# Regrouping the small attention matmuls of a packed-attention and mixture-of-experts kernel by array tile

## The chip, the cores and the metric

One core of one Trainium2 chip runs the whole program. The metric is the time of one execution in device microseconds, lower is better. In the profile PE is TensorE's matmuls, PEld its weight loads, DVE VectorE, ACT ScalarE, POOL GpSimd and SP SyncE (here a queue of DMA issues). A line number after L is a line of the kernel before, unless the text says that it is one of the changed kernel.

## What is computed

```python
# per batch (8) and head (8): q, k, v are [576, 64], p is [32, 64]
p_packed = softmax(scale * p @ k.T) @ v                       # [32, 64]
x        = softmax(scale * q @ p_packed.T) @ p_packed         # [576, 64]
# x of all heads side by side: 4608 tokens of 512
xn, en   = x / (norm(x) + 1e-6), emb / (norm(emb) + 1e-6)     # emb: 8 experts of 512
logits   = xn @ en.T / tau
e        = argmax(logits)                                     # one expert per token
out      = softmax(logits)[e] * (relu(x @ w1[e]) @ w2[e])     # w1 [512,1024], w2 [1024,512]
```

## The kernel before

**Work per batch.** The program goes through the 8 batches. For each it guesses one expert for the whole batch from the packed values (`pair_sums`, `guess_products`, `guess`), loads that expert's w1 and w2, and runs the feed-forward part (`ffn`) on all 576 tokens with it; tokens that want another expert would be done in a loop at the end, which these inputs do not enter.

**Groups and tiles.** The 8 heads of a batch form two groups g of four. Column tile `c` (32 of the array's 128 columns) holds head `head(g, c) = c ^ g`. A matmul's `tile_position` says which rows and columns of the array it takes; an operand of 64 rows and 32 columns leaves room for eight such matmuls side by side, one of 128 rows and 32 columns for four.

**The attention of one batch**, in TensorE's order:

1. `key_scores` (L266): scores of the 32 packed rows of each head against 576 keys; `key_max` on DVE, `key_exp` on ACT give `p1[g]`, 128 rows (4 heads of 32) by 576 keys.
2. `p1_turn` (L374): five transposes per group, four of 128 keys and one of the last 64, here called the odd block. `p1_evac` copies the four blocks (L385 on ACT, or L387 on DVE) and the odd one (L388 on DVE) to `p1T[g]`.
3. `pack_values` (L394): for each group 5 blocks by 4 heads, weights `p1T`, moving 64 columns of v. The odd block uses 64 rows of the array, the others 128.
4. `pair_rows` on DVE (L406), `pair_turn` on PE (L423), a copy to `x.T` (L508), `pair_sums` on DVE (L447), `packed_rows` on ACT (L420).
5. `row_logits` (L434): four matmuls of 128 rows, 64 columns, 8 moving columns: the packed rows against the normalised experts; `logits_out` (L443) copies them behind the packed values in `ppf`. `query_scores` (L266 again), and `guess_products` (L454): four matmuls of one weight column and 8 moving columns, added up in PSUM. `guess` reads the sum on DVE (L554 to L558), and the index it finds sends w1 (L841) and w2 (L849) on POOL's queue.
6. `att2`: softmax over the packed rows (L599 unpacks the scores out of PSUM, then L604 and on), `route` (L708) builds the logits of each token.

**What sets the order.** Every engine runs its own instructions in program order. The order is written by hand: `ffn` is a generator, and after each of its steps the attention of the next batch takes one step, so that L266, L374, L394, L423, L434 and L454 of batch b + 1 stand between L974 (first layer) and L1002 (second layer) of batch b, and L708 stands before and among the L1020 that follow. Batch 0's attention is written out in `begin` and has nothing to stand between. Batch 1 goes the `tight` way, with fewer steps: there the four transposes of its queries (L296 on DVE) come among the last steps of its packing, for the other batches earlier.

**PSUM and SBUF.** Pool `pb` has two tiles of two banks (key scores, turned blocks, values, query scores, routing take them in turn), pool `ps` four of one bank. SBUF tiles are named by tag: `p1` had two buffers of 576 columns, `st` two of the same size, used at the start for the embeddings (`emb_sb`, `esq`, `en_sb`).

Of the kernel before, what the change touches and what calls it, by code (L numbers as in the profile page):

```python
# [17 lines left out]
P = 128  # L18
# [5 lines left out]
def kernel(  # L24
# [174 lines left out]

    RUNS = ((0, 5), (5, 5), (10, 4), (14, 4))  # L200

    def load_v(b, g):
        t = sb.tile([P, NC5 * HB * D], F32, name="nat", tag="nat", bufs=6)
        t = t.rearrange("p (h w) -> p h w", h=HB)
        s = v[b, g * HB : (g + 1) * HB].rearrange("h (i c) d -> i h (c d)", c=NCB)
        for a, (at, n) in enumerate(RUNS):
# [75 lines left out]

    def flip(t, key, e=0):
# [3 lines left out]
        if key:  # L287
# [20 lines left out]
    def keys(x, nat, pn, more=None, scaled=False):  # L308
# [3 lines left out]
        for r in range(NPR):  # L312
            x.kT[r] = flip(nat(r), True)
            if more and r == NPR - 1:
# [64 lines left out]

    def p1_evac(x, g, pt, pl, w=512, spare=None):  # L380

        x.p1T[g] = sb.tile([P, NC5, P], F32, name="p1T", tag=spare or "p1T", bufs=NF if spare else 2)
        t = x.p1T[g][:, 0:4].rearrange("p a b -> p (a b)")
# [6 lines left out]
    def pack_values(x, g, vt, pt):  # L390
        for c in range(NC5):
            r = rows(c)
            for at in range(HB):
                nc.tensor.matmul(  # L394
                    pt[32 * at : 32 * at + 32, 0:D],
                    x.p1T[g][:r, c, 32 * at : 32 * at + 32],
                    vt[:r, head(g, at), c, :],
                    start=(c == 0),
                    stop=(c == NC5 - 1),
                    tile_position=(0, 32 * at),  # L400
                )

# [55 lines left out]
    def att1(x, nat, tight=False, rest=False):  # L458
# [5 lines left out]

        turned = []

        def turn(g):
            turned.append(pb.tile([P, 1024], F32, name="pt", tag="pb"))
            p1_turn(x, g, turned[g], turned[g][:, 512:])

        def evac(g, w=512):
            p1_evac(x, g, turned[g], turned[g][:, 512:], w)

        def values():
            pt = pb.tile([P, 1024], F32, name="pt", tag="pb")
            for g in range(NG):
                pack_values(x, g, nat(2 * NPR + g), pt[:, g * D : g * D + D])
            return [pt[:, g * D : g * D + D] for g in range(NG)]

        def pack():  # L480
            pack_tiles(x)
            if not tight:
                yield
            for g in range(NG):
                turn(g)
            for g in range(NG):
                evac(g, 0 if tight and g else 512)
                if not tight:
# [28 lines left out]
            pt = ps.tile([P, 512], F32, name="pu", tag="pf")  # L517
            row_logits(x, pt)
            if tight:
                guess_products(x, pt)  # L520
            query_scores(x)
            if not tight:
                if not rest:
                    guess_products(x, pt)
                yield
            logits_out(x, pt, nc.vector.tensor_copy)
            yield
# [22 lines left out]

    def guess(x, engine=mybir.EngineType.Pool):
        m8 = sm.tile([1, 8], F32, name="m8", tag="m8")
        idx = sm.tile([1, 8], U32, name="idx", tag="idx")
# [565 lines left out]
    def begin():  # L1119
# [8 lines left out]
        nc.scalar.dma_start(itau, tau.broadcast_to([P, 1]))  # L1128
        kn = [load_whole(k, g) for g in range(NG)]
        vn = [load_v(0, g) for g in range(NG)]  # L1130
        qn = [load_whole(q, g) for g in range(NG)]
# [52 lines left out]
        pack_values(x, 0, vn[0], po[0])  # L1184
        p1_evac(x, 1, pt, pt[:, 512:], 512, "w2s")
        pair_rows(x, 0, po[0])
# [347 lines left out]
```

## Time and profile before

| | |
|---|---|
| median of 3 runs (lowest to highest) | 423.76 us (423.23 to 425.24) |
| profiled execution | 422.4 us, its span 420.8 us |
| PE busy | 410.4 us, 98% of the span |
| DVE, ACT, POOL busy | 304.5, 217.7, 141.8 us (72%, 52%, 34%) |
| DMA | 88.36 MB, mean 210 GB/s |
| granted TensorE clock, mean | 0.994 |

The span runs from the first to the last instruction; 1.6 us of the execution lie around it. All rows below are of this one execution. "Busy" of PE is a union of overlapping matmuls; matmuls are pipelined, and so what one group costs TensorE is best read as the time from its first start to the first start of the next group.

### The profile page before, as it was taken

To read this page: it belongs to the slowest core of one execution; us is meant where nothing else is said; L and a number is where in the kernel's file an instruction comes from. 1 tells how busy PE (TensorE), PEld (TensorE's weight loads), DVE (VectorE), ACT (ScalarE), POOL (GpSimd) and SP (SyncE) were. 2 spreads that over 40 slices of the span, in tenths; PEclk is the share of its full clock that TensorE was granted. 3 is DMA by queue.
4 is the path that set the end of the run, shared out by engine and by line. 5 is a ranking of instruction groups with operands and counts; after the bars stand their busy time and mean duration, and the time that the engine had idled before them with its cause. 6 is when DMAs were issued, how large, how long until landed. Compare 5 with 4: busy or idle time off the path is not lost.

```text
span 420.8 us, 12550 instructions
## 1 busy us (share of the span) xinstructions
PE 410.4 (98%) x4780; PEld 346.1 (82%) x4781; DVE 304.5 (72%) x931; ACT 217.7 (52%) x651; POOL 141.8 (34%) x193
## 2 busy tenths in 40 slices
PE   8899999999999999999999999999999999999993
PEld 3647898698977999688986989779986989879983
DVE  5467788678975899758986889858988589637220
ACT  2556733973446653574536734476436744466300
POOL 2457646660405321251404404143212614044000
PEclk9899999999999999999999999999999999999999
DMA  8999889975999779786999379973898404640022
GB/s 225 304 289 308 240 249 276 278 188 145 263 306 248 198 215 365 213 222 187 292 338 232 82 211 333 273 200 101 255 369 218 135 2 177 226 101 14 2 64 57
DMA packets 48024, 88.36 MB, mean 210 GB/s; under 512 B 11020, under 2 KB 29516, under 8 KB 47956
## 3 DMA queue, kind: packets, MB, share of 16 engines
q1 hardware_dynamic: 39460, 57.83, 50.7%
q0 software_dynamic: 7968, 29.43, 20.5%
q8 instruction: 40, 0.66, 0.7%
q10 hardware_dynamic: 528, 0.21, 0.2%
q14 instruction: 28, 0.23, 0.2%
HBM read 78.00 MB, written 9.44 MB: 208 GB/s over the span
## 4 chain that ended last, share of the span: by engine, by line
PE 93%; DMA 3%; DVE 1%; ACT 1%; issue 0%; SPq 0%; DVEq 0%; ACTq 0%
PE pf L1002 27%; PE pf L974 23%; PE pf L1020 22%; PE pt L708 4%; PE pt L266 4%; PE pt L890 3%; PE pt L394 3%; DMA nat<-in_k 2%; PE pt L374 2%; PE pf L1144 1%; DMA w2r<-in_moe_w 1%; PE pt L244 1%; PE pf L1227 1%; PE pu L434 1%; PE pu L454 1%; PE pu L423 0%
## 5 line engine op out<-in xcount | busy, mean ns | idle before, releaser
L866 POOL TENSOR_TENSOR w2s<-w2r,w2s 128x512 fp32r<-128x512 f32 x64 | 81.8, 1286 | 121.1 <-ACT w2s L865 117.6
L1002 PE MATMUL pf<-hT,w2s 128*128 128x320 f32 x768 | 118.8, 312 | 0.0
L1002 PEld LDWEIGHTS pf<-hT,w2s 128*128 128x128 f32 x768 | 113.0, 188 | 1.5 <-issue 0.5
L974 PE MATMUL pf<-AT,G 128*128 128x288 f32 x720 | 103.9, 298 | 0.1
L974 PEld LDWEIGHTS pf<-AT,G 128*128 128x128 f32 x720 | 97.3, 188 | 4.8 <-issue 2.8
L1020 PE MATMUL pf<-w2s,hT 128*128 128x512 f32 (+1 forms) x408 | 94.5, 385 | 0.0
L1020 PEld LDWEIGHTS pf<-w2s,hT 128*128 128x128 f32 x408 | 72.1, 188 | 19.9 <-issue 5.0
L977 DVE SCALAR_TENSOR_TENSOR hT<-pf,hT 128x288 fp32r<-128x288 f32 x128 | 56.3, 446 | 33.2 <-ACT hT L976 33.2
L976 ACT ACTIVATE hT<-pf 128x288 fp32r<-128x288 f32 x128 | 51.2, 415 | 39.6 <-PE pf L974 38.2
L735 ACT ACTIVATE scr<-pt 128x256 f32<-128x256 f32 (+1 forms) x80 | 29.3, 382 | 30.9 <-DVE lg L726 30.9
L865 ACT CAST w2s<-w2r 128x512 fp32r<-128x512 f32 x64 | 39.2, 625 | 7.6 <-issue 7.2
L841 POOL DMA_DIRECT2D w1t<-in_moe_w x14 | 10.7, 766 | 80.0 <-DVE st L591 76.1
L827 ACT COPY gt<-gate 32x2 f32<-32x2 f32 (+1 forms) x128 | 24.6, 192 | 6.9 <-DVE gate L812 5.3
L906 DVE TENSOR_TENSOR G<-pt,G 128x512 fp32r<-128x512 f32 x28 | 18.6, 689 | 8.9 <-ACT G L905 8.5
L1306 DVE STREAM_TRANSPOSE ot<-pf 128x320 f32<-128x320 f32 x32 | 16.0, 501 | 12.2 <-PE pf L1002 11.0
L612 ACT ACTIVATE st<-st 128x576 f32<-128x576 f32 (+1 forms) x17 | 11.2, 658 | 23.5 <-issue 16.6
L629 ACT CAST AT<-at 128x576 fp32r<-128x576 f32 x15 | 10.1, 673 | 23.1 <-DVE at L626 23.1
L1289 ACT ACTIVATE o<-pf,gate 128x512 f32<-128x512 f32 (+1 forms) x17 | 11.3, 666 | 20.3 <-issue 14.3
L296 DVE STREAM_TRANSPOSE kt<-nat 128x576 f32<-128x576 f32 x28 | 21.3, 763 | 0.1
L905 ACT CAST G<-pt 128x512 fp32r<-128x512 f32 x28 | 15.8, 588 | 9.5 <-PE pt L890 7.6
L849 POOL DMA_DIRECT2D w2r<-in_moe_w x28 | 19.7, 711 | 0.0
L708 PEld LDWEIGHTS pt<-ppf,at 32*64 32x64 f32 x1152 | 15.0, 130 | 4.8 <-issue 4.3
(178 smaller groups left out, 476.1 us busy)
## 6 DMA issues: line engine op xcount, KB each, us to landing
nat<-in_k SPq DMA_DIRECT2D x112, 140.0 KB, 3.5
nat<-in_q SPq DMA_DIRECT2D x112, 140.0 KB, 4.3
w1t<-in_moe_w POOLq DMA_DIRECT2D x14, 1024.0 KB, 8.8
w2r<-in_moe_w POOLq DMA_DIRECT2D x28, 512.0 KB, 12.4
nat<-in_v SPq DMA_DIRECT2D x32, 160.0 KB, 4.4
out<-ot SPq DMA_DIRECT2D x28, 160.0 KB, 3.8
nat<-in_v SPq DMA_DIRECT2D x32, 128.0 KB, 4.4
out<-o SPq DMA_DIRECT2D x62, 64.0 KB, 2.3
```

The lines of the kernel that those rows point to most:

```text
L296: nc.vector.transpose(kt.rearrange("p (n i) -> p n i", i=32), t)
L708: nc.tensor.matmul(pts[h // 2][64 * (n % 2) : 64 * (n % 2) + 64, at : at + XW], x.at[32 * h : 32 * h + 32, g, 64 * n : 64 * n + 64], x.ppf ...
L735: nc.scalar.activation(scr[:r], views[m][:r, :, c - c0, :D], AF.Square, accum_out=sss[:r, m, c : c + 1],)
L827: copy(dst[32 * a : 32 * a + 32, k : k + HB * (n - 1) + 1 : HB], src[32 * k : 32 * k + 32, NCT : NCT + n],)
L849: queue.dma_start(t, w2e[:, 2 * i : 2 * i + 2, :])
L865: nc.scalar.copy(hi, raw)
L866: eng.tensor_tensor(out=lo, in0=raw, in1=hi.bitcast(F32), op=ALU.subtract)
L974: nc.tensor.matmul(pf[:, :HS], w, r, start=(n == 0), stop=(n == len(ops) - 1))
L976: nc.scalar.activation(hT[:, 0, f, cs], pf[:, :HS], AF.Relu)
L977: nc.vector.scalar_tensor_tensor(out=hT[:, 1, f, cs], in0=pf[:, :HS], scalar=0.0, in1=hT[:, 0, f, cs].bitcast(F32), op0=ALU.max, op1=ALU.s ...
L1002: nc.tensor.matmul(pf[:, : S - TL], x.w2s[f][:, m, mt * P : mt * P + P], hT[:, a, f, TL:], start=(n == 0), stop=(n == len(ops) - 1),)
L1020: nc.tensor.matmul(pf[:, :w], hT[:, a, f, c * P : (c + 1) * P], x.w2s[f][:, m, at : at + w], start=(f == 0 and i == 0), stop=(f == NF - 1 ...
```

## The change

Six things, without their purpose:

- **Odd blocks.** `p1` of both groups lies in one tile `pa` of 2 x 576 columns. For group 1 the keys are put with the odd block first (`flip(..., odd_first)`, and v loaded in runs that match), so that the two odd blocks are neighbours: `turn_all` makes nine transposes of 128 instead of ten, and `evac_odd` copies both odd blocks at once to `p1o`. `evac_main` copies the others.
- **Values.** `pack_all` issues the 32 matmuls of 128 rows of both groups in one run (the groups to two banks), then the 8 odd ones, group 0 in the array's upper 64 rows, group 1 in the lower.
- **Row logits** come as eight matmuls of 64 rows and 32 columns just ahead of `query_scores`, in the same array tiles, and go to unused columns of the query scores' first PSUM tile (`x.rl`).
- **Guess.** `pair_sums` also multiplies the sums by the experts on DVE (`terms`), one matmul with a column of ones sums over the rows, after `query_scores` for every batch, and `guess` adds four pieces on DVE (`gsum`).
- **Batch 0** keeps `p1_turn`, `pack_values`, `row_logits` and `guess_products`; its odd blocks of `p1T` and v have 64 rows of zeros (memsets on POOL), and its matmuls use all 128 rows.
- **Buffers.** Batch 0's `p1` takes tag `st`, its `p1T` tag `w2s`.

```diff
-    RUNS = ((0, 5), (5, 5), (10, 4), (14, 4))
+    RUNS = (((0, 5), (5, 5), (10, 4), (14, 4)), ((0, 4), (4, 4), (8, 5), (13, 5)))
...
+        if runs is RUNS[0] and isinstance(b, int) and b == 0:
+            nc.gpsimd.memset(t[64:, :, HB * D :], 0.0)
...
+        if key and odd_first:
+
+            ko = kt[:, 64:].rearrange("p (n a i) -> p a n i", a=4, i=32)
+            ti = t[:, 8:].rearrange("p (a n) d -> p a n d", a=2)
+            nc.vector.transpose(ko[:, :2], t[:, :8].rearrange("p (a n) d -> p a n d", a=2))
+            nc.vector.transpose(ko[:, 2:], ti[:, :, :4])
+            nc.vector.transpose(kt[:, :64].rearrange("p (a i) -> p a i", i=32), ti[:, :, 4])
...
+            if not hf:
+                x.rl = pt.rearrange("p (g w) -> p g w", g=NG)[:, :, HS : HS + E]
+        for g in range(NG):
+            for c in range(HB):
+                h = head(g, c)
+                nc.tensor.matmul(
+                    x.rl[32 * c : 32 * c + 32, g],
+                    half_rows(x.T, h)[:, g * P + 32 * c : g * P + 32 * c + 32],
+                    half_rows(enT[:, 2 * g + h // 2], h),
+                    start=True,
+                    stop=True,
+                    tile_position=(64 * (h % 2), 32 * c),
+                )
...
-        x.p1[g] = sb.tile([P, S], F32, name="p1", tag="p1", bufs=2)
+        if x.b == 0:
+            x.p1[g] = sb.tile([P, S], F32, name="p1", tag="st", bufs=2)
+        else:
+            if not g:
+                x.pa = sb.tile([P, NG, S], F32, name="pa", tag="p1", bufs=1)
+            x.p1[g] = x.pa[:, g]
...
+    def turn_all(x):
+        x.turned = [pb.tile([P, 1024], F32, name="pt", tag="pb") for _ in range(NG)]
+        flat = x.pa.rearrange("p g s -> p (g s)")
+        for n in range(2 * HB + 1):
+            pt, at = (x.turned[0], n * P) if n < HB else (x.turned[1], (n - 5) % 5 * P)
+            nc.tensor.transpose(pt[:, at : at + P], flat[:, n * P : n * P + P], ident)
...
+    def pack_all(x, vts, pts):
+        for c in range(HB):
+            for g in range(NG):
+                for at in range(HB):
+                    nc.tensor.matmul(
+                        pts[g][32 * at : 32 * at + 32],
+                        x.p1T[g][:, c, 32 * at : 32 * at + 32],
+                        vts[g][:, head(g, at), c, :],
+                        start=(c == 0),
+                        stop=False,
+                        tile_position=(0, 32 * at),
+                    )
+        for g in range(NG):
+            r = slice(64 * g, 64 * g + 64)
+            for at in range(HB):
+                nc.tensor.matmul(
+                    pts[g][32 * at : 32 * at + 32],
+                    x.p1o[r, 32 * at : 32 * at + 32],
+                    vts[g][r, head(g, at), HB, :],
+                    start=False,
+                    stop=True,
+                    tile_position=(64 * g, 32 * at),
                 )
...
+        x.terms = sm.tile([P, NPR, E], F32, name="terms", tag="terms", bufs=1)
+        nc.vector.tensor_tensor(
+            out=x.terms, in0=x.total.unsqueeze(2).broadcast_to([P, NPR, E]), in1=enT, op=ALU.mult
+        )
+
+    def guess_sums(x, pt):
+        x.parts = pt[:1, : NPR * E]
+        nc.tensor.matmul(
+            x.parts, ones, x.terms.rearrange("p n e -> p (n e)"), start=True, stop=True
+        )
...
-            row_logits(x, pt)
-            if tight:
-                guess_products(x, pt)
             query_scores(x)
+            if not rest:
+                guess_sums(x, ps.tile([P, 512], F32, name="pu", tag="pf"))
...
-            logits_out(x, pt, nc.vector.tensor_copy)
+            nc.vector.tensor_copy(x.ppf[:, :, D:], x.rl)
...
+        if x.b:
+            x.guess = sm.tile([1, E], F32, name="gsum", tag="gsum", bufs=1)
+            nc.vector.tensor_reduce(
+                x.guess.unsqueeze(2), x.parts.rearrange("p (n e) -> p e n", n=NPR),
+                axis=AX.X, op=ALU.add,
+            )
```

Where this puts instructions, at three places. First TensorE in the attention of batch 3 (its rows are alike for batches 2 to 7), before; `ident` is the identity, `pu` and `pt` are PSUM tiles, the figures behind the names are columns and rows, and a row counts matmuls as written, of which the trace shows two records each except for transposes and the feed-forward ones:

```order
L374 MATMUL pt<-ident,p_1543 128x128 x4
L374 MATMUL pt<-ident,p_1543 64x128
L374 MATMUL pt<-ident,p_1572 128x128 x4
L374 MATMUL pt<-ident,p_1572 64x128
L974 MATMUL pf<-AT,G 128x288 x24
L394 MATMUL pt<-nat,p1T 32x64 x40
```

and further on

```order
L1002 MATMUL pf<-hT,w2s 128x320 x8
L434 MATMUL pu<-enT,T 64x8 x4
L266 MATMUL pt<-kt,T 32x288 x16
L454 MATMUL pu<-enT,total 1x8 x4
L1002 MATMUL pf<-hT,w2s 128x320 x76
```

The same stretch of the changed kernel (line numbers of the changed kernel):

```order
L434 MATMUL pt<-ident,pa 128x128 x9
L1042 MATMUL pf<-AT,G 128x288 x24
L448 MATMUL pt<-nat,p1T 32x64 x32
L459 MATMUL pt<-nat,p1o 32x64 x8
L1042 MATMUL pf<-AT,G 128x288 x18
L488 MATMUL pu<-ident,pp_2589 128x128
L488 MATMUL pu<-ident,pp_2591 128x128
L1042 MATMUL pf<-AT,G 128x288 x6
L1070 MATMUL pf<-hT,w2s 128x320 x8
L351 MATMUL pt<-enT,T 32x8 x8
L269 MATMUL pt<-kt,T 32x288 x16
L522 MATMUL pu<-terms,ones 1x32
```

The stretches between are as long as before (24, 18, 6 and 8 feed-forward matmuls); one transpose and three guess matmuls are gone, four logit matmuls are new and have moved into the scores' tiles.

Second VectorE in batch 1, the `tight` one, from the last query transpose but one to the first step of the softmax, before:

```order
L296 STREAM_TRANSPOSE kt<-nat 128x576
L447 TENSOR_REDUCE total<-T 128x4
L296 STREAM_TRANSPOSE kt<-nat 128x576
L443 COPY ppf<-pu 128x2x8
L554 MAX m_966<-pu 1x8
L555 MAX_INDEX idx<-m_966,pu 1x8
L557 CAST gi<-idx 1x1
L558 TENSOR_SCALAR sels<-ecol,gi 1x8
L599 STREAM_TRANSPOSE st<-pt 128x288 x4
```

and in the changed kernel:

```order
L306 STREAM_TRANSPOSE kt<-nat 128x576
L512 TENSOR_REDUCE total<-T 128x4
L516 TENSOR_TENSOR terms<-total,enT 128x32
L306 STREAM_TRANSPOSE kt<-nat 128x576
L588 COPY ppf<-pt 128x2x8
L616 TENSOR_REDUCE gsum<-pu 1x8
L622 MAX m_973<-gsum 1x8
L623 MAX_INDEX idx<-m_973,gsum 1x8
L625 CAST gi<-idx 1x1
L626 TENSOR_SCALAR sels<-ecol,gi 1x8
L667 STREAM_TRANSPOSE st<-pt 128x288 x4
```

`terms` now stands ahead of the last query transpose, and `gsum`, which reads the guess matmul behind the query scores, stands ahead of the four unpacking transposes of the softmax.

Third ScalarE at the start of batch 0, with what each instruction waits for; L359 and L387 are the two exponentials of `key_exp`. Before:

```order
L359 ACTIVATE p_252,sums<-pt,mx 128x576 [waits DVE_49]
L359 ACTIVATE p_263,sums<-pt,mx 128x576 [waits DVE_49]
L385 COPY p1T<-pt 128x512 [waits PE_49]
L149 ACTIVATE en_sb<-emb_sb,enrm 8x512 [waits DVE_49,Activation_49]
L156 ACTIVATE enT<-pf,itau 128x32 [waits PE_49]
```

and in the changed kernel:

```order
L387 ACTIVATE p_258,sums<-pt,mx 128x576 [waits DVE_49,Activation_49]
L387 ACTIVATE p_269,sums<-pt,mx 128x576 [waits DVE_49,PE_49,Activation_49]
L412 COPY p1T<-pt 128x512 [waits PE_49]
L149 ACTIVATE en_sb<-emb_sb,enrm 8x512 [waits DVE_49,Activation_49]
L156 ACTIVATE enT<-pf,itau 128x32 [waits PE_49]
```

The order is the same; the second exponential now also waits for TensorE, because the two `p1` of batch 0 share one buffer of tag `st` (the other still holds `emb_sb`, which L149 reads later).

## Rows read from the trace of the kernel before

**Rows 1.** Windows: each engine's busy time in a stretch, granted clock, DMA share, GB/s.

```profile
core 0: us, PE busy (x) PEld busy (x) DVE busy (x) ACT busy (x) POOL busy (x), PEclk, DMA share, GB/s
16.00:19.50 3.50, 3.50 (x31) 2.70 (x29) 1.28 (x5) 1.81 (x4) 0.00 (x0) 0.51 0.94 242
139.00:188.00 49.00, 49.00 (x591) 42.28 (x590) 39.38 (x115) 26.51 (x81) 14.83 (x17) 1.00 0.83 247
```

**Rows 2.** Timeline of PE, batch 3: start, length, line, operands, records.

```profile
139.03 1.25 PE L374 MATMUL pt<-ident,p 128*128 128x128 f32 x10
140.04 3.45 PE L974 MATMUL pf<-AT,G 128*128 128x288 f32 x24
143.42 1.73 PE L394 MATMUL pt<-nat,p1T 128*32 128x64 f32 x80
145.08 2.66 PE L974 MATMUL pf<-AT,G 128*128 128x288 f32 x18
...
149.89 0.41 PE L434 MATMUL pu<-enT,T 128*64 128x8 f32 x8
150.23 1.20 PE L266 MATMUL pt<-kt,T 64*32 64x288 f32 x32
151.36 0.34 PE L454 MATMUL pu<-enT,total 128*1 128x8 f32 x8
151.63 0.56 PE L1002 MATMUL pf<-hT,w2s 128*128 128x320 f32 x2
```

**Rows 3.** Timelines of PE in windows of 3 to 10 ns within batch 3.

```profile
143.50 0.44 PE L394 MATMUL pt<-nat,p1T 128*32 128x64 f32 x17
143.83 0.43 PE L394 MATMUL pt<-nat,p1T 128*32 128x64 f32 x8
144.00 0.32 PE L394 MATMUL pt<-nat,p1T 64*32 64x64 f32 x8
144.25 0.43 PE L394 MATMUL pt<-nat,p1T 128*32 128x64 f32 x16
...
151.53 0.17 PE L454 MATMUL pu<-enT,total 128*1 128x8 f32 x1
```

**Rows 4.** Timeline of PE, batch 3's second routing stage.

```profile
168.59 1.21 PE L708 MATMUL pt<-ppf,at 32*64 32x72 f32 x80
169.72 0.50 PE L1020 MATMUL pf<-w2s,hT 128*128 128x512 f32 x1
```

**Rows 5.** Timeline of all engines, batch 1 around its query scores.

```profile
51.34 0.37 ACT L508 COPY T<-pu 128x256 f32<-128x256 f32 x1
...
51.75 0.42 DVE L447 TENSOR_REDUCE total<-T 128x4 f32<-128x256 f32 x1 [0.40 <-ACT T L508]
...
52.08 0.77 DVE L296 STREAM_TRANSPOSE kt<-nat 128x576 f32<-128x576 f32 x1
...
52.41 0.41 PE L434 MATMUL pu<-enT,T 128*64 128x8 f32 x8
...
53.02 1.20 PE L266 MATMUL pt<-kt,T 64*32 64x288 f32 x32
...
53.22 0.15 DVE L554 MAX8 m<-pu 1x8 f32<-1x8 f32 x1
...
53.85 0.22 DVE L558 TENSOR_SCALAR sels<-ecol,gi 1x8 f32<-1x8 f32 x1
...
54.32 1.58 DVE L599 STREAM_TRANSPOSE st<-pt 128x288 f32<-128x288 f32 x4 [0.25 <-PE pt L266]
...
56.70 0.42 PE L708 MATMUL pt<-ppf,at 32*64 32x72 f32 x20
```

**Rows 6.** Timeline of all engines, batch 0's packing.

```profile
10.62 0.74 PE L374 MATMUL pt<-ident,p 128*128 128x128 f32 x5 [0.58 <-POOL rq_t L110]
...
10.89 0.74 ACT L359 ACTIVATE p<-pt,mx 128x576 f32<-128x576 f32 x1 [0.42 <-DVE mx L354]
...
12.58 0.59 ACT L385 COPY p1T<-pt 128x512 f32<-128x512 f32 x1 [0.86 <-PE pt L374]
```

**Rows 7.** DVE in batch 2: a timeline row, and a group of instructions.

```profile
100.65 0.42 DVE L447 TENSOR_REDUCE total<-T 128x4 f32<-128x256 f32 x1
...
L388 DVE COPY p1T<-pt 64x128 f32<-64x128 f32 x2 | 0.5, 266 | 0.0
```

**Rows 8.** Timelines of POOL and PE: the loads of batch 2's w1, its first reader.

```profile
106.27 1.58 POOL L841 DMA_DIRECT2D w1t<-in_moe_w  x2 [12.69 <-DVE st L591]
...
125.91 1.09 PE L890 MATMUL pt<-w1t,T 64*32 64x512 f32 x16
```

More of the change, by code (lines that the diff above doesn't have):

```diff
@@ L197, in load_whole @@
         return t
-    RUNS = ((0, 5), (5, 5), (10, 4), (14, 4))
+    RUNS = (((0, 5), (5, 5), (10, 4), (14, 4)), ((0, 4), (4, 4), (8, 5), (13, 5)))
     def load_v(b, g):
+        runs = RUNS[0 if isinstance(b, int) and b == 0 else g]
         t = sb.tile([P, NC5 * HB * D], F32, name="nat", tag="nat", bufs=6)
         t = t.rearrange("p (h w) -> p h w", h=HB)
+        if runs is RUNS[0] and isinstance(b, int) and b == 0:
+            nc.gpsimd.memset(t[64:, :, HB * D :], 0.0)
         s = v[b, g * HB : (g + 1) * HB].rearrange("h (i c) d -> i h (c d)", c=NCB)
-        for a, (at, n) in enumerate(RUNS):
+        for a, (at, n) in enumerate(runs):
             nc.sync.dma_start(
@@ L281, in split, with flip @@
         eng.tensor_tensor(out=dst[1], in0=src, in1=dst[0].bitcast(F32), op=ALU.subtract)
-    def flip(t, key, e=0):
+    def flip(t, key, e=0, odd_first=False):
         kt = sb.tile([P, S], F32, name="kt", tag="kq", bufs=8)
         t = t.rearrange("p (c e d) -> p c e d", e=2, d=32)[:, :, e]
-        if key:
+        if key and odd_first:
[4 more added lines that the diff above has]
+            nc.vector.transpose(kt[:, :64].rearrange("p (a i) -> p a i", i=32), ti[:, :, 4])
+        elif key:
             ko = kt[:, :512].rearrange("p (n a i) -> p a n i", a=4, i=32)
@@ L312, in keys @@
         for r in range(NPR):
-            x.kT[r] = flip(nat(r), True)
+            x.kT[r] = flip(nat(r), True, odd_first=r >= NPR // 2)
             if more and r == NPR - 1:
@@ L378, in p1_turn, with p1_evac @@
             )
-    def p1_evac(x, g, pt, pl, w=512, spare=None):
-        x.p1T[g] = sb.tile([P, NC5, P], F32, name="p1T", tag=spare or "p1T", bufs=NF if spare else 2)
+    def p1_evac(x, g, pt, pl, w=512):
         t = x.p1T[g][:, 0:4].rearrange("p a b -> p (a b)")
@@ L391, in pack_values @@
         for c in range(NC5):
-            r = rows(c)
             for at in range(HB):
@@ L395, in pack_values @@
                     pt[32 * at : 32 * at + 32, 0:D],
-                    x.p1T[g][:r, c, 32 * at : 32 * at + 32],
-                    vt[:r, head(g, at), c, :],
+                    x.p1T[g][:, c, 32 * at : 32 * at + 32],
+                    vt[:, head(g, at), c, :],
                     start=(c == 0),
@@ L400, in pack_values, with evac_main, evac_odd @@
                     tile_position=(0, 32 * at),
+                )
[5 more added lines that the diff above has]
+            nc.tensor.transpose(pt[:, at : at + P], flat[:, n * P : n * P + P], ident)
+    def evac_main(x, g, copy):
+        x.p1T[g] = sb.tile([P, HB, P], F32, name="p1T", tag="p1T", bufs=2)
+        copy(x.p1T[g].rearrange("p a b -> p (a b)"), x.turned[g][:, :512])
+    def evac_odd(x):
+        x.p1o = sb.tile([P, P], F32, name="p1o", tag="p1o")
+        nc.vector.tensor_copy(x.p1o, x.turned[1][:, 512 : 512 + P])
+    def pack_all(x, vts, pts):
[4 more added lines that the diff above has]
+                        pts[g][32 * at : 32 * at + 32],
+                        x.p1T[g][:, c, 32 * at : 32 * at + 32],
+                        vts[g][:, head(g, at), c, :],
[13 more added lines that the diff above has]
+                    tile_position=(64 * g, 32 * at),
                 )
@@ L463, in queries @@
                 yield
[L465 to L472, printed above, removed]
         def values():
             pt = pb.tile([P, 1024], F32, name="pt", tag="pb")
-            for g in range(NG):
-                pack_values(x, g, nat(2 * NPR + g), pt[:, g * D : g * D + D])
-            return [pt[:, g * D : g * D + D] for g in range(NG)]
+            pts = [pt[:, g * 512 : g * 512 + D] for g in range(NG)]
+            pack_all(x, [nat(2 * NPR + g) for g in range(NG)], pts)
+            return pts
         def pack():
@@ L483, in pack @@
                 yield
+            turn_all(x)
+            evac_odd(x)
             for g in range(NG):
-                turn(g)
-            for g in range(NG):
-                evac(g, 0 if tight and g else 512)
+                evac_main(x, g, nc.vector.tensor_copy if tight and g else nc.scalar.copy)
                 if not tight:
@@ L516, in pack @@
                 yield from idle(2)
-            pt = ps.tile([P, 512], F32, name="pu", tag="pf")
-            row_logits(x, pt)
-            if tight:
-                guess_products(x, pt)
             query_scores(x)
+            if not rest:
+                guess_sums(x, ps.tile([P, 512], F32, name="pu", tag="pf"))
             if not tight:
-                if not rest:
-                    guess_products(x, pt)
                 yield
-            logits_out(x, pt, nc.vector.tensor_copy)
+            nc.vector.tensor_copy(x.ppf[:, :, D:], x.rl)
             yield
@@ L551, in guess @@
     def guess(x, engine=mybir.EngineType.Pool):
+        if x.b:
[3 more added lines that the diff above has]
+                axis=AX.X, op=ALU.add,
+            )
         m8 = sm.tile([1, 8], F32, name="m8", tag="m8")
@@ L1129, in begin @@
         kn = [load_whole(k, g) for g in range(NG)]
+        for g in range(NG):
+            x.p1T[g] = sb.tile([P, NC5, P], F32, name="p1T", tag="w2s", bufs=NF)
+            nc.gpsimd.memset(x.p1T[g][64:, HB], 0.0)
         vn = [load_v(0, g) for g in range(NG)]
@@ L1184, in begin @@
         pack_values(x, 0, vn[0], po[0])
-        p1_evac(x, 1, pt, pt[:, 512:], 512, "w2s")
+        p1_evac(x, 1, pt, pt[:, 512:], 512)
         pair_rows(x, 0, po[0])
```

## The prediction

> **What bounds the kernel now.** I read the busy shares first: TensorE is busy for 98% of the span, VectorE for 72%, the others less. Then the windows of one batch: in the 49.00 us that begin with batch 3's transposes TensorE is busy for all 49.00, at a granted clock of 1.00, and VectorE for 39.38 [rows 1]. So in the steady batches nothing waits for anything but TensorE, and what a group of matmuls takes there, from its first start to the next group's first start, goes into the time one for one. Only at the start is that otherwise: batch 0 has no feed-forward work to fill the gaps, and batch 1 is the tight one.
>
> **The transposes.** In batch 3 ten take 140.04 - 139.03 = 1.01 us [rows 2]. Nine should take 0.9: **-0.10** (the removed one is as wide in the array as the others but has half the rows to write, so -0.05 to -0.15).
>
> **The values.** They take 145.08 - 143.42 = 1.66 [rows 2], in four pieces [rows 3]: group 0's main blocks until 144.00, 0.58, its odd block until 144.25, 0.25, then the same for group 1, 0.58 and 0.25. Inside a main piece the quads (four matmuls side by side in the four column tiles, two records each) start 0.055 apart: the second at 143.50, the eighth at 143.83, six steps in 0.33. Eight quads at that pace are 0.44; the other 0.14 is lost where the array goes from 128-row to 64-row tiles and back. The change has one such passage instead of three inside the product. So I put group 0's main at 0.58 less what lies at its end, group 1's main at 0.44, and both odd groups, now in the two halves of the array's rows and free to run side by side, at 0.28: 0.58 + 0.44 + 0.28 = 1.31 with the rounding, **-0.35**. Bounds: if side by side costs as little as one group does, 0.25; if the 16 odd records go no faster than the eight-abreast ones of the routing, 80 in 1.13, 0.014 each [rows 4], the odd part is 0.25 + 8 x 0.014 = 0.36, and without any gain from the missing passages the whole is 1.42: -0.24 to -0.38.
>
> **The row logits.** Four of 128 rows take 150.23 - 149.89 = 0.34 [rows 2]. The eight of 64 rows (16 records) form two groups, each with several tiles side by side, and use the tiles that the scores use next, so no passage lies between. The nearest rows for such a group are the quads: the first costs 0.08 (143.42 to 143.50), a further one 0.055 [rows 2, 3]. That makes 0.135, **-0.20**. The upper price is every record by itself at the routing's 0.014 to 0.017, 0.22 to 0.27 [rows 4], so -0.07 to -0.23.
>
> One rule of the Trainium skill speaks against this part: the page "TensorEngine Tiling (Array Packing)", section Instruction Overhead, says that each matmul carries about 60 cycles of overhead, that one with a free dimension of 1 takes as long as one with 60, and that the tiling factor is not to be taken from a dimension that is already small. The moving side here has 8 columns, and the number of matmuls doubles. On one tile the trace agrees: the guess's 8-column records start (151.53 - 151.36) / 7 = 0.025 us apart [rows 2, 3]. By that, 16 records would cost 0.40, not 0.135, and the sum below would be 1.8 us smaller. Against it stand the quads, four records in 0.055, and the routing, both on tiles side by side, so I go by 0.135 and keep the other as a rival.
>
> **The guess.** Four matmuls take 151.63 - 151.36 = 0.27, of which seven steps are 0.17 and the way back to the feed-forward part 0.10 [rows 2, 3]. One matmul, two records of 32 columns, leaves 0.025 + 0.10, **-0.14** (0 to -0.20, since the passage from the scores' tiles to a one-column weight may dominate).
>
> **Sum for a batch:** 0.10 + 0.35 + 0.20 + 0.14 = **0.79 us** (0.36 to 0.96).
>
> **What is added elsewhere.** VectorE loses one odd copy (266 ns [rows 7]) and gains `terms` and `gsum`, each at most a `total` of 0.42 [rows 7] and more likely 0.2: +0.13 a batch, under the 9.6 us that VectorE has free. The expert's index comes 0.2 to 0.35 later, behind `gsum`; what hides it is that w1's issue at 106.27 has its first reader only at 125.91 [rows 8]. Without that cover it would cost those 0.35 in each batch. `pa` as one tile is read by all nine transposes at once and is written again a batch later. The evacuations have 3.4 us of feed-forward matmuls in front of the values [rows 2], and need two ScalarE copies of 0.59 [rows 6]. So batches 2 to 7 give 6 x 0.79 = **-4.75**.
>
> **Batch 1.** TensorE gains 0.45 ahead of the row logits, 0.20 in them, and the 0.27 of the guess now come behind the scores, so it reaches the scores 0.92 earlier, at 52.10 instead of 53.02, and their second quarter, the first to read the last query transpose, at 52.40 [rows 5]. That transpose began at 52.08 and ended at 52.85. `total` ahead of it waited 0.40 for ScalarE's copy of T; that wait may go, as the copy's inputs come earlier too, but `terms` (0.15) comes in between. So it ends at 52.60, with 0.17 of hand-over 52.77: TensorE waits 0.37; if the copy does not move, 0.77. I take **0.55**. Next late is the unpacking: behind `gsum` and the five steps of the guess (53.22 to 54.07, 0.85 [rows 5]), which before were over when the scores ended, the four unpacking transposes start about 0.95 later after the scores, at 54.32 - 0.37 + 0.13 + 0.95 = 55.03, and end at 56.61. The routing's matmuls (56.70 before [rows 5]) need those banks and are wanted at 56.46, so they wait another **0.3** (0 to 0.6). Batch 1: -0.79 + 0.55 + 0.3, about **0** (-0.9 to +0.6).
>
> **Batch 0.** Its second exponential ran at 10.89, beside the five transposes of 10.62 to 11.36 [rows 6]. Both `p1` now share a buffer, so it waits for the last of these: it starts at about 11.4, +0.5. ScalarE's copy at 12.58 waited 0.86 for the second transposes and moves along. Part of the delay is given back by the zero-filled odd blocks, which leave no change of tile in its two products (0.1 or so each). I take **+0.3** (0 to 0.5). The memsets on POOL lie before any reader.
>
> **Total:** -4.75 + 0 + 0.3 = -4.4. The profiled execution of 422.4 becomes 418.0. It lies 1.4 under the median of the three runs, 423.76, so the forecast for the median is **419.3 us**.
>
> **The rivals.** Half a per cent, 2.1 us, is what I count as telling a change from none: under 421.6 is faster, over 425.9 slower.
> - *Batch 1 does not stall.* TensorE is a little late everywhere before it, or the scheduler's other work fills the gaps: 0.85 less, **418.5**. For it speaks the 0.40 that `total` had to spare; against it the 0.92.
> - *Batch 1 stalls more,* because the late unpacking also holds up VectorE's later transposes of the tight batch: 1 us more, **420.3**.
> - *A record costs 0.025 wherever it stands.* Then the row logits are 0.06 dearer instead of 0.20 cheaper, 7 x 0.26: **421.1**. The page named above would have it so; the quads speak against it.
> - *The upper prices hold everywhere:* 6 x 0.36 = 2.2 gained, 0.4 lost in batch 1 and 0.5 in batch 0: -1.3, **422.5**, no change.
> - *The values wait for VectorE.* The one odd copy stands in VectorE's queue, and the 8 odd matmuls need it, now for both groups. It is wanted about 1 us after the values begin, at 144.4, with the transposes over at 140.04. VectorE must be 4.4 us late before anything is lost, and 5.4 before a batch loses the 0.95 that make the whole slower: 7 x (0.95 - 0.79) + 0.3 + batch 1's 0.85 is +2.3, **426.0**. VectorE's longest row here is 1.58 for four transposes [rows 5], and it has free time, so this is unlikely.
>
> **Chances.** Forecast 0.50, no stall 0.18, more stall 0.11, a record at 0.025 0.08, upper prices 0.08, VectorE 0.05 (in a milder form for 0.02, which ends as no change). Faster 0.87, the same 0.10, slower 0.03. The range 417.5 to 421.5 holds the first four and the scatter of each; the forecast's own is 418.3 to 420.2.
>
> **What would show it.** In a steady batch, first start to next first start: transposes 0.90, values 1.31, row logits 0.135, guess 0.13, and 48.2 us from one batch's transposes to the next instead of 49.0. In batch 1 a wait of TensorE inside the scores for the last query transpose, and one ahead of the routing for the unpacking. In batch 0 the second exponential at about 11.4. **What would make it wrong:** the stretch of 16.0 to 19.5 ran at a granted clock of 0.51, the lower of the two levels, with TensorE busy throughout [rows 1]; if the changed start makes that stretch longer or shorter, it moves the time by up to its own half, 1.7 us. A wait of TensorE in a steady batch, which has none now, would do so too.

## The result and the profile after

| | before | changed |
|---|---|---|
| median of 4 runs each (lowest to highest) | 423.74 us (423.23 to 425.24) | 418.88 us (418.14 to 420.78) |
| ratio, 95% interval | | 0.9893 [0.9862, 0.9925] |
| profiled execution, its span | 422.4, 420.8 us | 419.25, 417.6 us |

The medians differ by 4.9 us, the two profiled executions by 3.15. Why, is the main thing that the runs had to settle, since the steady batches went nearly as the prediction had it. First TensorE in batch 3 of the changed kernel, as a timeline (line numbers are now those of the changed kernel), beside [rows 2]:

```profile
139.94 1.14 PE L434 MATMUL pt<-ident,pa 128*128 128x128 f32 x9
140.84 3.44 PE L1042 MATMUL pf<-AT,G 128*128 128x288 f32 x24
144.21 1.10 PE L448 MATMUL pt<-nat,p1T 128*32 128x64 f32 x64
145.24 0.34 PE L459 MATMUL pt<-nat,p1o 64*32 64x64 f32 x16
145.51 2.67 PE L1042 MATMUL pf<-AT,G 128*128 128x288 f32 x18
...
150.32 0.25 PE L351 MATMUL pt<-enT,T 64*32 64x8 f32 x13
150.40 0.41 PE L269 MATMUL pt<-kt,T 64*32 64x288 f32 x1
...
150.45 1.20 PE L269 MATMUL pt<-kt,T 64*32 64x288 f32 x31
151.58 0.22 PE L522 MATMUL pu<-terms,ones 128*1 128x32 f32 x2
151.73 1.00 PE L1070 MATMUL pf<-hT,w2s 128*128 128x320 f32 x5
```

From first start to next first start: transposes 0.90, values 1.30, row logits and scores together 1.26, guess 0.15. The window of that batch, from its transposes to the next batch's, beside the second of [rows 1]:

```profile
core 0: us, PE busy (x) PEld busy (x) DVE busy (x) ACT busy (x) POOL busy (x), PEclk, DMA share, GB/s
139.94:188.03 48.09, 48.09 (x592) 41.69 (x590) 39.42 (x116) 26.29 (x81) 14.86 (x17) 1.00 0.83 249
```

TensorE still has no gap there, and VectorE is as busy as before. The transposes of before's batches 3 and 4 were 48.90 us apart (139.03 in [rows 2] to 187.93 below), now 48.09.

Batch 1 is another matter. Its timeline, TensorE and VectorE, beside [rows 5]; a bracket is idle time ahead of the row and what ended it:

```profile
51.83 0.42 DVE L512 TENSOR_REDUCE total<-T 128x4 f32<-128x256 f32 x1 [0.40 <-ACT T L574]
...
52.28 0.19 DVE L516 TENSOR_TENSOR terms<-total,enT 128x32 f32<-128x32 f32 x1
...
52.58 0.41 PE L269 MATMUL pt<-kt,T 64*32 64x288 f32 x1
...
53.71 0.78 DVE L306 STREAM_TRANSPOSE kt<-nat 128x576 f32<-128x576 f32 x1 [1.23 <-DMA nat<-in_q]
...
54.54 1.16 PE L269 MATMUL pt<-kt,T 64*32 64x288 f32 x20 [1.22 <-DVE kt L306]
55.63 0.22 PE L522 MATMUL pu<-terms,ones 128*1 128x32 f32 x2
...
56.87 1.56 DVE L667 STREAM_TRANSPOSE st<-pt 128x288 f32<-128x288 f32 x4
```

The scores last from 52.58 to 55.63, 3.05 us against 1.18 in batch 3 (150.40 to 151.58). The last query transpose waited 1.23 of that for its load; the rest is taken up below. In batch 0 the second exponential waits for the transposes of the first, and starts at 11.52 instead of 10.89 [rows 6]:

```profile
11.52 0.74 ACT L387 ACTIVATE p<-pt,mx 128x576 f32<-128x576 f32 x1 [0.97 <-PE pt L402]
```

The transposes of batches 1, 2 and 4 divide the two profiled executions into stretches. Before:

```profile
43.76 1.25 PE L374 MATMUL pt<-ident,p 128*128 128x128 f32 x10
...
90.04 1.25 PE L374 MATMUL pt<-ident,p 128*128 128x128 f32 x10
...
187.93 1.25 PE L374 MATMUL pt<-ident,p 128*128 128x128 f32 x10
```

Changed:

```profile
44.14 1.24 PE L434 MATMUL pt<-ident,pa 128*128 128x128 f32 x9
...
91.81 1.14 PE L434 MATMUL pt<-ident,pa 128*128 128x128 f32 x9
...
188.03 1.14 PE L434 MATMUL pt<-ident,pa 128*128 128x128 f32 x9
```

So the profiled pair is made up like this: up to batch 1's transposes 0.38 lost (43.76 to 44.14), from there to batch 2's 1.39 lost (90.04 to 91.81, less the 0.38), in the six batches after that 4.9 gained.

### The profile page after: what moved, and what is told of

It is laid out like the page before. It is cut to its first block, busy times and chain, and to the rows that moved or that the text cites. A ratio compares the mean times of both kernels' runs of the same rounds, so it can differ in the third digit from the quotient of the medians.

```text
span 417.6 us, 12561 instructions
## 1 busy us (share of the span) xinstructions
PE 404.9 (97%) x4787; PEld 341.7 (82%) x4788; DVE 304.7 (73%) x938; ACT 217.3 (52%) x651; POOL 143.1 (34%) x197
## 4 chain that ended last, share of the span: by engine, by line
PE 87%; DMA 5%; DVE 3%; ACT 1%; SPq 1%; issue 1%; POOL 0%; DVEq 0%; ACTq 0%; POOLq 0%
PE pf L1070 27%; PE pf L1042 22%; PE pf L1088 22%; PE pt L269 4%; PE pt L776 4%; PE pt L958 3%; DMA nat<-in_k 2%; PE pt L448 1%; PE pt L434 1%; DMA nat<-in_q 1%; DMA w2r<-in_moe_w 1%; DMA pn<-in_p 1%; DVE hT L1045 1%; DVE kt L301 0%; DVE kt L302 0%
## 5 line engine op out<-in xcount | busy, mean ns | idle before, releaser
L909 POOL DMA_DIRECT2D w1t<-in_moe_w x14 | 10.7, 768 | 82.6 <-DVE st L659 75.9
```

## Experiments: the price of each term in a steady batch

Single times scatter by a microsecond and more, but the distance between the transposes of two steady batches does not: 48.09 and 48.10 in two executions of the changed kernel (139.94 to 188.03 above, 139.44 to 187.54 in a second). These four kernels are read by it, one execution each.

**rl_old.** In batches 1 to 7 the row logits go back to four matmuls and a PSUM tile of their own.

```diff
...
-                nc.tensor.matmul(
-                    x.rl[32 * c : 32 * c + 32, g],
...
+            pr = ps.tile([P, 512], F32, name="pu", tag="pf")
+            row_logits(x, pr)
             query_scores(x)
...
```

> Only the row logits undone: four matmuls of 128 rows and 64 columns into a PSUM tile of their own ahead of the query scores, as in the kernel before; values, guess and the rest as changed. Read by the distance between the transposes of one batch and the next (48.09 us in the changed kernel, 48.90 before), since the time of one execution scatters by a microsecond. If sixteen records on tiles side by side are as cheap as the trace after has it (0.13 for the group against 0.34), 48.29. If the matmuls cost by their number and the gain came from elsewhere, 48.03 to 48.09.

Measured, TensorE's timeline:

```profile
140.47 1.14 PE L421 MATMUL pt<-ident,pa 128*128 128x128 f32 x9
...
188.76 1.14 PE L421 MATMUL pt<-ident,pa 128*128 128x128 f32 x9
```

48.29: the row logits are worth 0.20, all of it by themselves. The edit undoes their form (eight of 64 rows) and their array tiles together, so it does not say which of the two gives it. (The batch before was 1.43 longer, most of it one wait of 1.18 in its routing that the trace puts down to nothing but issue; its cause stays open, and it makes the single time, 422.05, of no use.)

**val_group.** The value matmuls in the old order, everything else as changed.

```diff
-        for c in range(HB):
-            for g in range(NG):
+        for g in range(NG):
+            for c in range(HB):
...
-        for g in range(NG):
             r = slice(64 * g, 64 * g + 64)
```

> Only the order of the value matmuls undone: group 0's 16 of 128 rows, its 4 of 64, then group 1's, in the same PSUM banks and with the same transposes as in the changed kernel. If the change of array tiles between 128 and 64 rows is what cost, together with the odd groups running one after the other, the product takes 1.66 again and the distance of batches is 48.45. If the gain came from the groups lying in two PSUM banks, or from the shared odd copy, it stays at 48.09.

```profile
139.96 1.14 PE L434 MATMUL pt<-ident,pa 128*128 128x128 f32 x9
...
144.22 0.65 PE L448 MATMUL pt<-nat,p1T 128*32 128x64 f32 x32
144.81 0.32 PE L458 MATMUL pt<-nat,p1o 64*32 64x64 f32 x8
145.06 0.65 PE L448 MATMUL pt<-nat,p1T 128*32 128x64 f32 x32
145.64 0.32 PE L458 MATMUL pt<-nat,p1o 64*32 64x64 f32 x8
145.88 2.67 PE L1041 MATMUL pf<-AT,G 128*128 128x288 f32 x18
...
188.41 1.14 PE L434 MATMUL pt<-ident,pa 128*128 128x128 f32 x9
```

The distance is 48.45 and the product 1.66, piece for piece that of before [rows 3] (0.59, 0.25, 0.58, 0.24). So it is the order by array tiles that gives the 0.36; the second PSUM bank and the shared copy give TensorE nothing. By pieces, the main blocks took 1.17 here and 1.03 in the changed kernel (144.21 to 145.24), the odd ones 0.49 and 0.27 (145.24 to 145.51): some 0.14 comes with the fewer passages, 0.22 with the odd groups side by side.

**rl_twice.** The row-logit loop runs twice, same result.

```diff
-        for g in range(NG):
+        for g in range(NG) if x.b == 1 else list(range(NG)) * 2:
```

> In batches 2 to 7 the eight row-logit matmuls are issued twice, with the same result; it measures the disputed cost by itself. By the spacing of records on tiles side by side in the trace after (two groups of eight at 0.055) the distance of batches grows by 0.11 to 48.20. If a record costs 0.025 wherever it stands, by 0.40 to 48.49.

```profile
139.09 1.14 PE L434 MATMUL pt<-ident,pa 128*128 128x128 f32 x9
...
149.47 0.34 PE L351 MATMUL pt<-enT,T 64*32 64x8 f32 x32
149.69 1.29 PE L269 MATMUL pt<-kt,T 64*32 64x288 f32 x32
...
187.38 1.14 PE L434 MATMUL pt<-ident,pa 128*128 128x128 f32 x9
```

48.29, 0.20 more for 16 records, and neither number was right: a second pass costs 0.0125 a record. That is half of what one of the guess's cost on a single tile, 0.025 [rows 2, 3], and near the routing's 0.014 [rows 4], which the prediction had as its upper price. The first pass is cheaper than the second: row logits and scores together take 1.26 in the changed kernel and the scores alone 1.13 in before, which leaves 0.13 for the first 16 records. Why the second pass costs more is not shown; it uses the array tiles and the PSUM columns that the first has just used.

**guess_old.** Four guess matmuls behind the scores, no `terms`, no `gsum`.

```diff
...
-                guess_sums(x, ps.tile([P, 512], F32, name="pu", tag="pf"))
+                guess_products(x, ps.tile([P, 512], F32, name="pu", tag="pf"))
...
```

> Only the guess undone: four matmuls of one weight column added up in PSUM behind the query scores, no terms and no gsum on VectorE. If one product with 32 columns instead of four with 8 is worth what the trace after shows (0.149 against 0.275), the distance of batches is 48.22. If VectorE's two added instructions cost the steady batches anything, it is less than that. In batch 1, without terms ahead of the last query transpose and gsum behind the scores, the scores wait 0.2 us less.

```profile
138.73 1.14 PE L434 MATMUL pt<-ident,pa 128*128 128x128 f32 x9
...
186.97 1.14 PE L434 MATMUL pt<-ident,pa 128*128 128x128 f32 x9
```

48.24, and 48.22 for the batch before: 0.13 to 0.15 for the guess, and VectorE's two added instructions cost a steady batch nothing. In batch 1 the scores took 1.50 (52.85 to 54.35). The three parts undone add up to 0.69 to 0.71 of the 0.81; the rest, 0.10 to 0.12, fits the transposes' 0.11 in the rows, which no run undid by itself.

## Experiments: batch 1 and the head

Three theories stood for the 3.05 us of batch 1's scores. A: the change itself brings the query load late, since batch 0's guess and all that SP's queue issues behind it come 0.4 us later. B: VectorE's order, with `terms` ahead of the last query transpose. C: the load's landing scatters, in either kernel.

**again.** The changed kernel once more.

> The changed kernel once more, unchanged. It tells what of batch 1's loss is of the kernel and what of the one execution profiled. In that execution the query scores of batch 1 took 3.05 us from their first start to the guess matmul's (52.58 to 55.63) where other batches take 1.13, because VectorE's last query transpose waited 1.23 us for its load. Theory A (the load is late because the guess of batch 0, and with it everything that the DMA queue issues behind it, comes 0.4 us later): the same wait again, 1 to 1.5 us, and a ratio to the kernel before of about 0.990. Theory C (the load was late by chance): the wait differs by more than 0.5 us, down to the 0.7 that the order on VectorE alone would leave. Steady batches 48.09 us apart by both.

Median of 6 runs 419.39 us (418.49 to 421.29), ratio 0.9912 [0.9885, 0.9938]. This time the load was in time:

```profile
53.17 0.78 DVE L306 STREAM_TRANSPOSE kt<-nat 128x576 f32<-128x576 f32 x1
...
53.28 0.41 PE L269 MATMUL pt<-kt,T 64*32 64x288 f32 x1
...
53.34 1.83 PE L269 MATMUL pt<-kt,T 64*32 64x288 f32 x31
55.09 0.22 PE L522 MATMUL pu<-terms,ones 128*1 128x32 f32 x2
```

The transpose follows `terms` at once, and the scores take 1.81, not 3.05. So, read from the rows, 0.6 to 0.7 of the wait belongs to the order on VectorE, and 1.2 to that one execution.

**before_again.** The kernel before once more, without an edit.

> The kernel before once more, for a second profile of its batch 1. Its first profile had the last query transpose of batch 1 begin at 52.08 with no wait for its load, and the query scores took 1.13 us. If the load is late by chance in either kernel, it may wait here too; the distance of its steady batches is 48.90 again. If the changed kernel alone brings the load late, the scores of batch 1 take 1.13 to 1.2 us.

```profile
52.35 0.78 DVE L296 STREAM_TRANSPOSE kt<-nat 128x576 f32<-128x576 f32 x1 [1.77 <-DMA nat<-in_q]
...
54.09 0.78 DVE L296 STREAM_TRANSPOSE kt<-nat 128x576 f32<-128x576 f32 x1 [0.66 <-DMA nat<-in_q]
...
53.48 0.35 PE L454 MATMUL pu<-enT,total 128*1 128x8 f32 x8 [0.73 <-DVE total L447]
53.76 0.70 PE L266 MATMUL pt<-kt,T 64*32 64x288 f32 x12
54.93 1.16 PE L266 MATMUL pt<-kt,T 64*32 64x288 f32 x20 [0.47 <-DVE kt L296]
56.02 2.62 PE L1002 MATMUL pf<-hT,w2s 128*128 128x320 f32 x16
```

The kernel before has the late load too, on its last two query transposes, and took 424.73 here against 422.4 in [rows 5]'s execution. So the load can be late without the change, and the profile that the prediction was made from shows batch 1 at its best. Theory A falls also by the kernels of the last section, whose head is the changed one: in none of the four did the last query transpose of batch 1 wait for its load.

**own_p1, sums_late, own_late** and **own_late2** (the same kernel as own_late, run again). Two edits, alone and together. Batch 0's `p1` in `pa`:

```diff
-        if x.b == 0:
-            x.p1[g] = sb.tile([P, S], F32, name="p1", tag="st", bufs=2)
-        else:
-            if not g:
-                x.pa = sb.tile([P, NG, S], F32, name="pa", tag="p1", bufs=1)
-            x.p1[g] = x.pa[:, g]
+        if not g:
+            x.pa = sb.tile([P, NG, S], F32, name="pa", tag="p1", bufs=1)
+        x.p1[g] = x.pa[:, g]
```

and `total` and `terms` of batch 1 one step later, behind the last query transpose:

```diff
-            if not rest:
+            if not rest and not tight:
                 pair_sums(x)
             if tight:
-                yield
+                yield; pair_sums(x)
```

> Batch 0's p1 goes into pa, as in the other batches, so that its second exponential no longer waits for TensorE's transposes. Theory A: the second exponential starts at about 10.9 instead of 11.52, w1's first issue of batch 0 at about 17.1 instead of 17.65, everything behind it comes 0.4 us earlier, and the last query load of batch 1 too, so that the wait inside the scores falls from 1.9 us to 1.5 or less: 0.4 to 0.9 us less in all. Theory B (batch 1's loss is VectorE's order, with terms ahead of the last query transpose): the head's 0.4 us comes back and the wait stays. Theory C: the head gains and batch 1 scatters.

> In batch 1 alone total and terms are computed behind the last query transpose instead of ahead of it; nothing else. Theory A: the transpose still waits for its load, at about 53.7, so the wait inside the scores stays, and the time is within 0.3 us of the changed kernel. Theory B: the transpose starts 0.6 us earlier and the wait falls by as much.

> Both edits together: batch 0's p1 in pa, and batch 1's total and terms behind the last query transpose. If load and order are both limits, one behind the other, this gives more than the sum of the two alone: the wait inside batch 1's scores falls under 0.7 us and the time is 1 to 1.6 us under the changed kernel, about 417.5. If only the load counts it equals the kernel with p1 in pa alone; if only the order, that with the late sums less 0.4 us.

> Batch 0's p1 in pa and batch 1's total and terms behind the last query transpose, once more: the kernel as before, since its times scattered (416.95 to 422.17). With order and head both mended, what is left of batch 1's wait is the load's: the scores take 1.2 us where the load is in time and up to 3 where it is not. Median 418 to 418.5, a ratio of 0.987 to 0.990.

| kernel | median (runs) | ratio to before | wait for the last query load | scores of batch 1 |
|---|---|---|---|---|
| changed, first profile | 418.88 (4) | 0.9893 | 1.23 us | 3.05 us |
| again | 419.39 (6) | 0.9912 [0.9885, 0.9938] | none | 1.81 |
| own_p1 | 417.96 (6) | 0.9868 [0.9845, 0.9891] | 0.76 | 2.59 |
| sums_late | 419.41 (6) | 0.9899 [0.9868, 0.9931] | 2.10 | 2.87 |
| own_late | 418.47 (5) | 0.9905 [0.9869, 0.9941] | 0.45 | 1.22 |
| own_late2 | 417.92 (6) | 0.9862 [0.9826, 0.9899] | 0.83 | 1.60 |

The last two columns are of the one profiled execution of each; the wait counts from when VectorE comes free. (In own_p1 the trace names a later load, `pn`, as what ended the wait; by the times of the semaphores the query load landed 0.12 before the transpose began.) In own_late the second exponential waits for its maximum alone, and the scores follow a transpose that stands ahead of `total`:

```profile
10.87 0.74 ACT L387 ACTIVATE pa<-pt,mx 128x576 f32<-128x576 f32 x1 [0.42 <-DVE mx L377]
...
51.38 0.78 DVE L306 STREAM_TRANSPOSE kt<-nat 128x576 f32<-128x576 f32 x1 [0.45 <-DMA nat<-in_q]
...
52.09 0.41 PE L269 MATMUL pt<-kt,T 64*32 64x288 f32 x1
...
53.31 0.22 PE L522 MATMUL pu<-terms,ones 128*1 128x32 f32 x2
```

Of the head, theory A had this right: own_late's w1 issue was at 17.13 instead of 17.65, and its batch 1 began 0.49 earlier (43.65), in own_late2 0.39. In own_p1's profile, the slowest of its six runs (420.65), the exponential came early too (11.01), but the w1 issue waited 0.9 for a query load and stood at 18.16, not at the 17.1 expected, and batch 1 began at 45.95.

The order came out as theory B had it. In each of the twelve profiled executions in which the scores were held up, they end 1.91 to 1.93 after the last query transpose begins (in own_late 51.38 to 53.31). So they end early only if that transpose begins early, and it begins when VectorE is free and the load is there, whichever comes last. In own_late and own_late2 it began 0.71 and 0.32 ahead of the scores' first start, in **again** 0.11, behind `total` and `terms`: with the sums moved the scores took 1.22 and 1.60 against 1.81. In sums_late it began 0.95 after that start, held by its load, and the edit could show nothing.

The times alone settle less. Both edits together gave medians of 418.47 and 417.92, the first above the 417.5 expected, the second just under its 418 to 418.5; over all their 11 runs the median is 418.2, over all 10 of the changed kernel 419.2. The rows show 0.4 to 0.5 for the head and 0.2 to 0.6 for the order, but the intervals of the ratios overlap, and own_p1, with the head alone, is as fast (417.96). So that the two together gain 1.0 is likely rather than shown, and what the order adds to it does not show in the times.

**w2_act.** Both edits, and three of batch 0's four w2 transfers issued from ScalarE's queue.

```diff
-        load_w2(x, x.e)
+        load_w2(x, x.e, tiles=1)
...
+                elif c == "z":
+                    load_w2(bat[0], bat[0].e2, nc.scalar, 1)
```

> The same two edits, and three of the four transfers of batch 0's w2 are issued by ScalarE, 2 to 9 us later than SP issued them, instead of by SP ahead of the value and query loads of batch 1. If the query load is late because SP's queue stands behind w2's transfers (its last four value issues waited for them, 5.1 us in all), the last query load is issued at 40 to 43 us instead of 46.7 to 49.5, batch 1's scores take 1.2 us in every execution, the slow executions go, and the median is 417 or less. If the load is late because the DMA engines are full, the issue moves and the landing does not, and the median stays at 418 to 418.5. If w2 comes too late for its casts on ScalarE at 40 to 47 us, TensorE waits in the second layer instead and the time is 419 or more.

Median of 7 runs 419.36 us (417.60 to 421.58), ratio 0.9899 [0.9862, 0.9936]: no gain, and the last query load was issued at 48.60, no earlier than in the changed kernel (48.13). TensorE did not wait for w2 in the second layer either, the third case expected. The waits of SP's queue between 16 and 55 us (us in total, times, longest) and VectorE's transpose tell why:

```profile
SPq L210 <- DMA w2r<-in_moe_w: 5.5, 1, 5.5
...
53.31 0.78 DVE L306 STREAM_TRANSPOSE kt<-nat 128x576 f32<-128x576 f32 x1 [1.78 <-DMA nat<-in_q]
```

The value issues on SP went on waiting for w2, now for a transfer that ScalarE had issued, 5.5 us at a stretch. The edit did not take the queue out from behind w2, so it does not tell a late issue from full DMA engines. The semaphores in the packed trace tell a little more: a load raises its semaphore sixteen times, and its reader waits for the sixteenth. For the last query load the sixteenth came 1.49 after the fifteenth in the changed kernel's first profile (52.09, 53.58), 1.52 in sums_late, 1.68 in own_p1 and 1.09 in own_late; in the six executions without a wait it was 0.1 to 0.8, and in own_late2, w2_act and before_again, which waited too, 0.65 to 0.81. So part of what scatters is one piece of the load, and part is its issue, at 47.01 in the first profile of before and at 49.14 in before_again, though batch 1 began at the same time in both. Why that piece comes late stays open.

## Why the prediction was right, and where it was not

**The steady batches.** 0.81 a batch was measured where the sum said 0.79, for the stated reason: TensorE waits for nothing there. By term: transposes 0.11 (said 0.10), values 0.36 (0.35), row logits 0.20 (0.20), guess 0.13 to 0.15 (0.14). The 16 records of the row logits cost 0.13 where they stand, as the quads had it (0.135), but that price does not hold for 16 more (0.20, **rl_twice**). The rival in which every record costs 0.025 falls: it had the row logits 0.06 dearer. The Trainium skill, page "TensorEngine Tiling (Array Packing)", section Instruction Overhead, gives each matmul about 60 cycles of overhead, by an estimate 0.025 us at 2.4 GHz, and says not to take the tiling factor from a dimension that is already small. On one tile the trace agrees, with 0.025 from record to record; on eight tiles side by side 16 records cost 0.13 and 16 more 0.20, where that price gives 0.40.

**The values waiting for VectorE,** the slower rival, did not occur: 48.09 us without a gap.

**Batch 0.** +0.38 against the +0.3 taken, by the mechanism named: the exponential comes 0.63 later, the w1 issue 0.41 (17.65 instead of 17.24), and removing the shared buffer takes the exponential back to 10.87. But this execution is the lowest of the seven with that head: batch 1's transposes began 0.38 to 1.06 later than 43.76, with a median of 0.64, outside the 0 to 0.5 that the sum allowed. In **again**, the highest, most of the excess arises where TensorE reads w1, for which it waited 0.19 and 0.28 (the next stage began at 30.39, in the first profile at 29.73).

**Batch 1.** The wait inside the scores was put at 0.55 and is 0.63 to 0.68 when the load is in time (1.81 less 1.13 or 1.18). The copy of T did not move: `total` waited 0.41 for it in **again**, as before. That is the case priced at 0.77, of which the hand-over from transpose to scores, taken as 0.17, is only 0.05 (54.49 to 54.54). The 0.3 ahead of the routing was mis-sized: the unpacking did start late, at 56.87, 1.24 after the scores, but the routing's first matmuls did not wait for it, and its 80 records took 1.35 instead of 1.21, so about 0.14. What the prediction did not have at all is the load. "That transpose began at 52.08" took for granted that the load had landed, because the one trace of before shows no wait for it; in a second execution of before the last two query transposes waited 1.77 and 0.66, and in the executions above the last one between nothing and 2.10. From the first transposes of batch 1 to batch 2's, **again** shows what is left without it: 46.47 (44.82 to 91.29) against 46.28, and **rl_twice**, whose batch 1 is the changed kernel's, 46.43: a loss of 0.15 to 0.19 where "about 0" was said.

**The total.** -4.4 was said. The medians give -4.9 in the first comparison and -4.0 in the second, over all 10 runs of the changed kernel and 28 of before -4.1 (419.2 and 423.3); the two first profiles give -3.15. That the total came out so near is in part luck. The steady batches gave 0.02 a batch more than said and batch 0 took some 0.3 more, and the late load, which the sum did not have, lengthens some executions of either kernel, so that some of it falls out between two medians; how much is not shown. The profile of before, 422.4, was one of its fastest executions (28 runs lie between 422.36 and 426.39), among other things because batch 1 did not wait in it; that is why the step from it to the median was needed, and the prediction gave no reason for it.

The clock in the stretch from 16.0, feared for 1.7 us, moved little. **before_again** ran that stretch at 1.00, where the first profile of before had 0.51, and it reached its first w1 matmuls 1.19 earlier (21.06 instead of 22.25), but batch 1's transposes only 0.09 earlier:

```profile
27.41 1.91 PE L934 MATMUL pt<-w1t,tw 64*32 64x512 f32 x12 [0.26 <-DMA w1t<-in_moe_w]
...
43.67 1.25 PE L374 MATMUL pt<-ident,p 128*128 128x128 f32 x10
```

TensorE reads w1 in between, and w1 had been issued at the same time in both (17.25 and 17.24). The changed kernel's two profiles had 1.00 there too.

## What to carry to other kernels

Where one engine is busy all the time and nothing else is late, its rows give the gain to hundredths: take first start to first start, not the sum of durations, and look for places where the array goes from one tile shape to another and back. At the start of the program, where loads and engines are all near their limit, one trace is one draw: before a wait of zero goes into a sum, profile the kernel twice. And the price of a group where it stands need not be the price of one more such group (0.13 and 0.20 here): measure the one that the change needs.

## What was not expected of the hardware

A pair of passages between 128-row and 64-row tiles, with the odd groups run side by side, was worth 0.36 us of 1.66. Sixteen more records on eight tiles side by side cost 0.0125 us each although they start 0.007 apart (16 between 150.32 and 150.42); the first sixteen cost 0.13 in all. The landing of one and the same 4-issue load scatters widely from execution to execution of one program: from w2's first issue to SP's last value issue, which waits for w2's end, it took 10.7 us in the first profile of the changed kernel (28.83 to 39.54) and 9.1 in **again** (29.49 to 38.60), 9.3 in the first of before (28.45 to 37.73) and 11.9 in before_again (28.36 to 40.21), and with it the query loads behind. In the slow ones a single one of the last transfer's sixteen semaphore updates is late: 39.52 in the changed kernel, when the other fifteen were in by 37.36, against 38.58 and 38.45 in **again** (40.19 and 38.74 in before_again). And an issue on one engine's queue can wait for a transfer that another engine issued (5.5 us in w2_act), where both use one semaphore.
